# Linear attention plus gated FFN on one core: the V projection becomes a Gram product, gate/up becomes row-tiled, and every engine's order is written by hand

## The chip, the cores and the metric

The kernel runs on one core of one Trainium2 chip. The metric is device time in microseconds (us), the median of the runs of a kernel. Engines are named as the profile names them: PE (TensorE matmul), PEld (TensorE weight load), DVE (VectorE), ACT (ScalarE), POOL (GpSimd), SP (SyncE, which here issues the DMAs; SPq is its queue).

## The reference, cut to what matters

```python
x = A_x                                   # [1, 2048, 576] bf16
xn = layernorm(x)                         # no scale, no shift
q, k, v = heads(xn @ wqkv)                # 32 heads of 18 columns, D = 576
phi = lambda t: where(t > 0, t + 1, exp(t)) + 1e-6
kv  = einsum("bhsd,bhse->bhde", phi(k), v)        # per head 18 x 18
z   = einsum("bhsd->bhd", phi(k))
o   = (phi(q) @ kv) / (phi(q) @ z + 1e-6)
out = x + o @ wo + (gelu(xn @ w_gate) * (xn @ w_up)) @ w_down    # F = 4608
```

The feed-forward part is by far the larger: 576 x 4608 twice and 4608 x 576 once, for 2048 rows.

## The kernel before

The 2048 rows are 16 tiles of 128 (the K/V stage) and 4 chunks of 512 (all else). Each tile is normalised, transposed and projected to K and V; per-head products accumulate in two PSUM banks. Then come Q for all chunks, and for each chunk a gate/up stage and a down stage. A scheduler decides the order in which instructions of different parts stand on each engine, and pools hand out buffers and PSUM banks. In the code, phi of a value t comes in three steps: Relu of -t and Exp on ACT give exp(min(t, 0)), a max on DVE gives max(t, 0) plus the small constant, and an add joins them.

```python
def phi(ps_ap, out_ap, rows, cols, add_eng):
    e = awork.tile(...)
    nc.scalar.activation(out=e, in_=ps_ap, func=ACT.Relu, scale=-1.0)
    nc.scalar.activation(out=e, in_=e, func=ACT.Exp, scale=-1.0)
    a = awork.tile(...)
    nc.vector.tensor_scalar(out=a, in0=ps_ap, scalar1=0.0, scalar2=EPS_ATT, op0=ALU.max, op1=ALU.add)
    add_eng.tensor_tensor(out=out_ap, in0=e, in1=a, op=ALU.add)

def layernorm_transpose(n):
    # 2 bn_stats, bn_aggr on DVE; Ln, Exp on ACT -> rstd            [cut]
    nc.vector.tensor_scalar(out=xn[:, 0:D], in0=xt, scalar1=mv[:, 0:1], scalar2=rstd, subtract, mult)
    nc.vector.tensor_scalar(out=xn[:, D:DX], in0=xt[:, 512:D], ...)  # the tail, once more, 64 columns
    # 5 transposes on PE, one copy to xnT on DVE                     [cut]

def k_project(n):      # per half: 5 matmuls of 288 columns, then phi with the add on POOL
def v_project(n):      # per half: 5 matmuls of 288 columns, then a copy on ACT
def kv_accumulate(n, pk, v):   # 5 matmuls of at most 133 columns into kv_ps0, kv_ps1

for n in range(2, NS):
    if n + 1 < NS:
        layernorm_transpose(n + 1)
    pk = k_project(n)
    pending.append((n, pk, v_project(n)))
    if len(pending) > KV_SKEW:
        kv_accumulate(*pending.pop(0))
# [cut: the rest of kv, Q for 20 units of 5 matmuls of 512 columns]

class _GuBatch:                      # r = 2 blocks f of 128 columns of w_gate and w_up
    def full(self, first):           # rows 0..511 of the contraction, 128 rows each
        for i in range(self.r):
            for (pst, wsb) in ((self.g[i], self.wg), (self.u[i], self.wu)):
                for kt in range(4):
                    nc.tensor.matmul(pst[:], lhsT=wsb[:, kt, fcol], rhs=xnT[:, kt, self.cs], ...)
    def pairs(self, first):          # rows 512..575: g on rows 0..63 and u on rows 64..127 of the array
        for i in range(self.r):
            nc.tensor.matmul(self.g[i][:], lhsT=self.wr[0:64, fcol],   rhs=xnT[0:64, 4, self.cs], ...)
            nc.tensor.matmul(self.u[i][:], lhsT=self.wr[64:128, fcol], rhs=xnT[64:128, 4, self.cs], ...)

def gu_double_batch(sc, f0, r):
    a.full(True); a.pairs(False); a.geglu()      # [cut: allocation]
    b.pairs(True); b.full(False); b.geglu()
```

Of the kernel before, what the change touches and what calls it, by code (L numbers as in the profile page):

```python
# [12 lines left out]
PSUM = bass.MemoryType.PSUM  # L13

P = 128
S = 2048
# [3 lines left out]
DA = DH + 1  # L20
# [7 lines left out]
DX = D + 64  # L28
# [4 lines left out]
CW = 7 * DA  # L33
# [7 lines left out]
KV_SKEW = 2  # L41
# [14 lines left out]
def kernel(  # L56
# [15 lines left out]
    x_flat = A_x.flatten_outer_dims()  # L72
    out_flat = out.flatten_outer_dims()
    x_view = x_flat.rearrange("(n p) d -> p n d", p=P)
    out_view = out_flat.rearrange("(n p) d -> p n d", p=P)
# [4 lines left out]
    dwork = ctx.enter_context(tc.tile_pool(name="dwork", bufs=2))  # L80
    fpool = ctx.enter_context(tc.tile_pool(name="ffn", bufs=1))
    fwork = ctx.enter_context(tc.tile_pool(name="fwork", bufs=3))
    psum = ctx.enter_context(tc.tile_pool(name="psum", bufs=8, space=PSUM))

    def bank(name):
        return psum.tile([P, 512], F32, name=name, tag="ps")

    def bank_bf16(name):
        return psum.tile([P, 8, P], BF16, name=name, tag="ps")
# [3 lines left out]
    if NWARM:  # L93
        warm = bank("warm")
        for _ in range(NWARM):
            nc.tensor.matmul(warm[:, 0:P], lhsT=ident[:], rhs=ident[:], start=True, stop=True)
    eps_ln = const.tile([P, 1], F32, name="eps_ln")
    nc.vector.memset(eps_ln[:], EPS_LN)
    nc.scalar.preload_act_table_set("natural_log_exp_and_others")

# [5 lines left out]
    kv18 = persist.tile([P, NCH, CR], BF16, name="kv18")  # L106
    kvT = persist.tile([P, NCH, CR], BF16, name="kvT")

    hT = fpool.tile([P, NF, SC], BF16, name="hT")
# [4 lines left out]
    def load_gu_block(f0, r):  # L114
        c0, c1 = f0 * P, (f0 + r) * P
        w = r * P
        wg = wg_bufs.next()
        wu = wu_bufs.next()
        wr = wr_bufs.next()
        nc.sync.dma_start(wg[:, :, :w], B_w_gate[0:512, c0:c1].rearrange("(kt p) c -> p kt c", p=P))  # L120
        nc.sync.dma_start(wu[:, :, :w], B_w_up[0:512, c0:c1].rearrange("(kt p) c -> p kt c", p=P))
        nc.sync.dma_start(wr[0:64, :w], B_w_gate[512:576, c0:c1])
        last = nc.sync.dma_start(wr[64:128, :w], B_w_up[512:576, c0:c1])
        return wg, wu, wr, last

    attn_cm = tc.tile_pool(name="attn", bufs=1)
    apool = attn_cm.__enter__()
    awork_cm = tc.tile_pool(name="awork", bufs=3)
    awork = awork_cm.__enter__()
    asmall_cm = tc.tile_pool(name="asmall", bufs=4)  # L130
    asmall = asmall_cm.__enter__()

    x_src = {}

    def load_x(n0, cnt):
        if cnt == 1:
            t = awork.tile([P, D], BF16, name="xs", tag="xs", bufs=2)
            nc.sync.dma_start(t[:], x_view[:, n0, :])
            x_src[n0] = t[:]
        else:  # L140
            t = awork.tile([P, 4, D], BF16, name="xg", tag="xg", bufs=2)
            nc.sync.dma_start(t[:, :cnt, :], x_view[:, n0:n0 + cnt, :])
            for i in range(cnt):
                x_src[n0 + i] = t[:, i, :]

    wqkv_sb = apool.tile([P, KT, 3 * D], BF16, name="wqkv_sb")
    nc.vector.memset(wqkv_sb[64:128, 4, :], 0.0)

    def load_wqkv_main(c0, c1):
        nc.sync.dma_start(wqkv_sb[:, 0:4, c0:c1], A_wqkv[0:512, c0:c1].rearrange("(kt p) c -> p kt c", p=P))  # L150

    load_x(0, 1)
    load_x(1, 1)
    load_wqkv_main(D, D + HALF)
    nc.sync.dma_start(wqkv_sb[0:64, 4, D:3 * D], A_wqkv[512:576, D:3 * D])
    load_wqkv_main(D + HALF, 2 * D)
    load_x(2, 2)
    load_wqkv_main(2 * D, 2 * D + HALF)
    load_wqkv_main(2 * D + HALF, 3 * D)
    load_wqkv_main(0, D)  # L160
    nc.sync.dma_start(wqkv_sb[0:64, 4, 0:D], A_wqkv[512:576, 0:D])
    load_x(4, 4)
    X_LATER = {3: (8, 4), 7: (12, 4)}

    bmask = const.tile([P, 7, DA], F32, name="bmask")

    def build_bmask():
        nc.gpsimd.memset(bmask[:], 1.0)
        nc.gpsimd.affine_select(
            out=bmask[:], in_=bmask[:], compare_op=ALU.is_ge, fill=0.0,  # L170
            base=0, pattern=[[-DH, 7], [0, DA]], channel_multiplier=1,
        )
        nc.gpsimd.affine_select(
            out=bmask[:], in_=bmask[:], compare_op=ALU.is_ge, fill=0.0,
            base=DH - 1, pattern=[[DH, 7], [0, DA]], channel_multiplier=-1,
        )

    NVB = KV_SKEW + 2
    v_bufs = _Ring([apool.tile([P, H, DA], BF16, name=f"v{i}") for i in range(NVB)])
    pk_bufs = _Ring([apool.tile([P, D], BF16, name=f"pk{i}") for i in range(NVB)])  # L180
    for t in v_bufs.tiles:
        nc.gpsimd.memset(t[:, :, DH:DA], 1.0)

    kv_ps = [bank("kv_ps0"), bank("kv_ps1")]

    def kv_accumulate(n, pk, v):
        for c in range(NCH):
            rows = DH * HCH[c]
            q0 = DH * HOFF[c]
            nh = HCH[c]  # L190
            h0 = HOFF[c]
            b = c // 3
            col = (c - 3 * b) * CW
            first_in_bank = (n == 0 and c in (0, 3))
            nc.tensor.matmul(
                kv_ps[b][:rows, col:col + nh * DA], lhsT=pk[:, q0:q0 + rows],
                rhs=v[:, h0:h0 + nh, :].rearrange("p h e -> p (h e)"),
                start=first_in_bank, stop=(n == NS - 1 and c in (2, 4)), skip_group_check=True,
            )

    def phi(ps_ap, out_ap, rows, cols, add_eng):
        e = awork.tile([P, SC], F32, name="phi_e", tag="phi_e")
        nc.scalar.activation(out=e[:rows, :cols], in_=ps_ap, func=ACT.Relu, scale=-1.0)
        nc.scalar.activation(out=e[:rows, :cols], in_=e[:rows, :cols], func=ACT.Exp, scale=-1.0)  # L204
        a = awork.tile([P, SC], F32, name="phi_a", tag="phi_a")
        nc.vector.tensor_scalar(  # L206
            out=a[:rows, :cols], in0=ps_ap, scalar1=0.0, scalar2=EPS_ATT, op0=ALU.max, op1=ALU.add,
        )
        add_eng.tensor_tensor(out=out_ap, in0=e[:rows, :cols], in1=a[:rows, :cols], op=ALU.add)

    def layernorm_transpose(n):
        xt = x_src.pop(n)
        stats = asmall.tile([P, 2, nc.vector.BN_STATS_DIM], F32, name="stats")
        xr = xt.rearrange("p (a b) -> p a b", a=2)
        for a_ in range(2):
            nc.vector.bn_stats(out=stats[:, a_, :], in_=xr[:, a_, :])  # L216
        mv = asmall.tile([P, nc.vector.BN_AGGR_DIM], F32, name="mv")
        nc.vector.bn_aggr(out=mv[:], in_=stats[:])
        rstd = asmall.tile([P, 1], F32, name="rstd")
        nc.scalar.activation(out=rstd[:], in_=mv[:, 1:2], func=ACT.Ln, bias=eps_ln[:], scale=1.0)  # L220
        nc.scalar.activation(out=rstd[:], in_=rstd[:], func=ACT.Exp, scale=-0.5)
        xn = awork.tile([P, DX], BF16, name="xn")
        nc.vector.tensor_scalar(  # L223
            out=xn[:, 0:D], in0=xt, scalar1=mv[:, 0:1], scalar2=rstd[:],
            op0=ALU.subtract, op1=ALU.mult,
        )
        nc.vector.tensor_scalar(
            out=xn[:, D:DX], in0=xt[:, 512:D], scalar1=mv[:, 0:1], scalar2=rstd[:],
            op0=ALU.subtract, op1=ALU.mult,
        )  # L230
        tp = bank_bf16("tp_x")
        for kt in range(KT):
            nc.tensor.transpose(tp[:, kt, :], xn[:, kt * P:(kt + 1) * P], ident[:])  # L233
        nc.vector.tensor_copy(out=xnT[:, :, n * P:(n + 1) * P], in_=tp[:, 0:KT, :])  # L234

    def k_project(n):
        ts_ = slice(n * P, (n + 1) * P)
        pk = pk_bufs.next()
        for hf in range(2):
            ps_k = bank("ps_k")  # L240
            for kt in range(KT):
                nc.tensor.matmul(  # L242
                    ps_k[:, :HALF], lhsT=xnT[:, kt, ts_],
                    rhs=wqkv_sb[:, kt, D + hf * HALF: D + (hf + 1) * HALF],
                    start=(kt == 0), stop=(kt == KT - 1),
                )
            phi(ps_k[:, :HALF], pk[:, hf * HALF:(hf + 1) * HALF], P, HALF, nc.gpsimd)
        return pk

    def v_project(n):  # L250
        ts_ = slice(n * P, (n + 1) * P)
        v = v_bufs.next()
        for hf in range(2):
            ps_v = bank("ps_v")
            for kt in range(KT):
                nc.tensor.matmul(  # L256
# [7 lines left out]
            )  # L264
        return v

    layernorm_transpose(0)
    layernorm_transpose(1)
    pk0 = k_project(0)
    pk1 = k_project(1)  # L270
# [244 lines left out]
```

## Time and profile before

The first three runs gave a median of 545.75 us (544.07 to 546.41).

| stage of the profiled execution | length, us | what fills it |
|---|---|---|
| K/V tiles, until Q starts | 63.22 | from 40 to 60 us PE without a gap, at the end 3.01 a tile |
| Q | 21.58 | 100 matmuls, one every 0.216 |
| gate/up of chunk 0 | 74.76 | |
| gate/up of chunks 1, 2, 3 | 71.75, 71.70, 71.62 | |
| down of chunk 0, of the others | 41.79, 41.40 | |

The page of the kernel before, its parts on busy time (share of the span, number of instructions) and on the chain that ended last (share of the span by engine):

```profile
PE 528.8 (97%) x3371; PEld 311.4 (57%) x3403; DVE 258.0 (48%) x462; ACT 152.0 (28%) x329; POOL 67.8 (12%) x79
...
PE 92%; DMA 2%; DVE 2%; SPq 1%; issue 1%; POOL 0%; ACT 0%; POOLq 0%; ACTq 0%
```

PE is the bound. Only work taken off PE, or a gap between two of its instructions, can move the time.

The same by stage. Each line is a stretch, its length, the busy time of each engine with the number of instructions, the granted clock, the share of the DMA engines and GB/s:

```profile
core 0: us, PE busy (x) PEld busy (x) DVE busy (x) ACT busy (x) POOL busy (x), PEclk, DMA share, GB/s
0.00:63.22 63.22, 55.07 (x517) 45.31 (x517) 44.87 (x130) 41.50 (x129) 27.11 (x45) 0.95 0.47 125
63.22:84.80 21.58, 21.58 (x103) 13.12 (x102) 19.05 (x31) 19.35 (x34) 12.51 (x10) 1.00 0.00 1
84.80:159.56 74.76, 74.12 (x374) 32.43 (x380) 46.95 (x86) 28.92 (x57) 10.80 (x9) 1.00 0.73 207
159.56:201.35 41.79, 41.73 (x337) 32.85 (x337) 24.08 (x34) 0.69 (x2) 5.80 (x5) 1.00 0.13 37
201.35:273.10 71.75, 71.18 (x354) 30.23 (x361) 23.62 (x37) 20.51 (x36) 0.00 (x0) 1.00 0.51 145
```

In the K/V stage DVE (44.87) and ACT (41.50) have less to do than PE (55.07), but not much less.

The K/V stage in the chain of waits of the kernel before (start, length, engine, output, line, count):

```profile
47.86 1.23 PE ps_k L242 x10
49.09 1.23 PE ps_v L256 x10
...
50.87 1.23 PE ps_k L242 x10
52.09 1.23 PE ps_v L256 x10
```

From one K to the next are 3.01 us: K 1.23, V 1.23, and transposes and kv in the rest. The chain stays on PE: the other engines keep up.

Gate/up in the timeline of the kernel before (start, length, engine, line, operation, output<-inputs), where it changes from 64-row to 128-row matmuls:

```profile
212.85 0.38 PE L400 MATMUL g<-xnT,wr_135 64*128 64x512 bf16 x1
212.85 0.38 PE L402 MATMUL u<-xnT,wr_135 64*128 64x512 bf16 x1
213.07 0.38 PE L400 MATMUL g<-xnT,wr_135 64*128 64x512 bf16 x1
213.07 0.38 PE L402 MATMUL u<-xnT,wr_135 64*128 64x512 bf16 x1
213.38 1.04 PE L392 MATMUL g<-xnT,wg_127 128*128 128x512 bf16 x4
```

Two 64-row matmuls on different halves of the array start together, and such pairs follow each other every 0.22 us, as full matmuls do. But from the last pair to the first full matmul are 0.31 us. (The 0.38 us length is that of one matmul in the pipeline; the spacing of the starts is what a slot costs.)

### The profile page before, as it was taken

To read this page: it belongs to the slowest core of one execution; us is meant where nothing else is said; L and a number is where in the kernel's file an instruction comes from. 1 tells how busy PE (TensorE), PEld (TensorE's weight loads), DVE (VectorE), ACT (ScalarE), POOL (GpSimd) and SP (SyncE) were. 2 spreads that over 40 slices of the span, in tenths; PEclk is the share of its full clock that TensorE was granted. 3 is DMA by queue.
4 is the path that set the end of the run, shared out by engine and by line. 5 is a ranking of instruction groups with operands and counts; after the bars stand their busy time and mean duration, and the time that the engine had idled before them with its cause. 6 is when DMAs were issued, how large, how long until landed. Compare 5 with 4: busy or idle time off the path is not lost.

```text
span 542.6 us, 8817 instructions
## 1 busy us (share of the span) xinstructions
PE 528.8 (97%) x3371; PEld 311.4 (57%) x3403; DVE 258.0 (48%) x462; ACT 152.0 (28%) x329; POOL 67.8 (12%) x79
## 2 busy tenths in 40 slices
PE   5999999999999999999999999999999999999997
PEld 4788764444457774444477744444677644445775
DVE  5996598877248613333288123323683123323101
ACT  3677797223330003223200013223100122322000
POOL 1445465101002100000011000000021000000000
PEclk8999999999999999999999999999999999999999
DMA  8920003897840114554511035545301245540000
GB/s 251 251 78 2 1 2 95 254 257 211 227 135 24 29 34 141 155 145 143 163 52 38 28 103 145 161 137 154 110 23 32 74 136 157 148 127 0 23 18 16
DMA packets 104851, 58.08 MB, mean 107 GB/s; under 512 B 5802, under 2 KB 104746, under 8 KB 104810
## 3 DMA queue, kind: packets, MB, share of 16 engines
q1 hardware_dynamic: 104810, 57.53, 37.6%
q8 instruction: 26, 0.43, 0.4%
q14 instruction: 15, 0.12, 0.1%
HBM read 55.15 MB, written 2.36 MB: 106 GB/s over the span
## 4 chain that ended last, share of the span: by engine, by line
PE 92%; DMA 2%; DVE 2%; SPq 1%; issue 1%; POOL 0%; ACT 0%; POOLq 0%; ACTq 0%
PE acc L468 26%; PE g L392 23%; PE u L392 23%; PE g L400 6%; PE ps_q L332 4%; PE acc L475 4%; DMA xg<-in_A_x_dram 2%; PE ps_k L242 2%; PE ps_v L256 2%; PE ps_den L365 1%; DVE stats L216 1%; DVE phi_a L206 1%; SPq L150 0%; PE tp_x L233 0%; DVE xn L223 0%
## 5 line engine op out<-in xcount | busy, mean ns | idle before, releaser
L409 DVE TENSOR_TENSOR hT<-u,gl 128x512 bf16<-128x512 f32 x144 | 95.7, 686 | 171.9 <-PE u L402 104.2
L408 ACT ACTIVATE gl<-g 128x512 f32<-128x512 f32 x144 | 81.9, 596 | 321.3 <-PE u L402 262.2
L468 PE MATMUL acc<-wd_sb,hT 128*128 128x288 bf16 x1152 | 146.4, 286 | 0.0
L468 PEld LDWEIGHTS <-hT 128*128 128x128 bf16 x1152 | 112.6, 98 | 30.0
L370 DVE RECIPROCAL den_sb<-den_sb 126x128 f32<-126x128 f32 (+3 forms) x100 | 68.0, 746 | 0.7
L371 POOL TENSOR_TENSOR pqT<-pqT,den_sb 126x512 bf16<-126x512 bf16 (+1 forms) x20 | 23.2, 1161 | 298.4 <-DVE den_sb L370 298.4
L480 DVE TENSOR_TENSOR res<-acc,xres 128x288 bf16<-128x288 f32 x32 | 14.6, 457 | 88.3 <-PE acc L475 88.3
L392 PE MATMUL u<-xnT,wu_133 128*128 128x512 bf16 x144 | 37.0, 379 | 0.1
L392 PE MATMUL u<-xnT,wu_131 128*128 128x512 bf16 x144 | 37.0, 379 | 0.1
L392 PE MATMUL u<-xnT,wu_130 128*128 128x512 bf16 x140 | 36.6, 379 | 0.3
L392 PE MATMUL g<-xnT,wg_128 128*128 128x512 bf16 x139 | 36.5, 379 | 0.2
L392 PE MATMUL g<-xnT,wg_127 128*128 128x512 bf16 x136 | 36.0, 380 | 0.7 <-issue 0.5
L392 PE MATMUL u<-xnT,wu_132 128*128 128x512 bf16 x140 | 36.4, 379 | 0.2
L392 PE MATMUL g<-xnT,wg_129 128*128 128x512 bf16 x137 | 36.1, 380 | 0.5 <-issue 0.3
L392 PE MATMUL g<-xnT,wg_126 128*128 128x512 bf16 x140 | 36.4, 379 | 0.1
L242 PE MATMUL ps_k<-wqkv_sb,xnT 128*128 128x288 bf16 x160 | 24.4, 304 | 6.0 <-DVE xnT L234 5.7
L204 ACT ACTIVATE phi_e<-phi_e 128x288 f32<-128x288 f32 (+2 forms) x52 | 26.7, 514 | 1.5
L475 PE MATMUL acc<-m_sb,pqT 126*128 126x288 bf16 (+1 forms) x160 | 24.9, 285 | 0.0
L392 PEld LDWEIGHTS <-wg_127 128*128 128x128 bf16 x144 | 12.6, 98 | 20.7 <-issue 7.9
L392 PEld LDWEIGHTS <-wg_129 128*128 128x128 bf16 x144 | 12.6, 98 | 20.4 <-issue 7.6
L392 PEld LDWEIGHTS <-wu_130 128*128 128x128 bf16 x144 | 14.1, 98 | 17.0
L392 PEld LDWEIGHTS <-wu_131 128*128 128x128 bf16 x144 | 14.1, 98 | 17.0
(96 smaller groups left out, 504.6 us busy)
## 6 DMA issues: line engine op xcount, KB each, us to landing
wd_sb<-in_B_w_down_dram SPq DMA_DIRECT2D x12, 432.0 KB, 4.0
wg_126<-in_B_w_gate_dram SPq DMA_DIRECT2D x18, 256.0 KB, 3.0
wu_130<-in_B_w_up_dram SPq DMA_DIRECT2D x18, 256.0 KB, 4.0
wg_127<-in_B_w_gate_dram SPq DMA_DIRECT2D x18, 256.0 KB, 3.0
wu_131<-in_B_w_up_dram SPq DMA_DIRECT2D x18, 256.0 KB, 3.3
wg_128<-in_B_w_gate_dram SPq DMA_DIRECT2D x18, 256.0 KB, 3.0
wu_132<-in_B_w_up_dram SPq DMA_DIRECT2D x18, 256.0 KB, 3.5
wg_129<-in_B_w_gate_dram SPq DMA_DIRECT2D x18, 256.0 KB, 3.1
```

Of the source, the lines that this page charges most:

```text
L204: nc.scalar.activation(out=e[:rows, :cols], in_=e[:rows, :cols], func=ACT.Exp, scale=-1.0)
L242: nc.tensor.matmul(ps_k[:, :HALF], lhsT=xnT[:, kt, ts_], rhs=wqkv_sb[:, kt, D + hf * HALF: D + (hf + 1) * HALF], start=(kt == 0), stop=(kt ...
L332: nc.tensor.matmul(ps[:rows, :], lhsT=wqkv_sb[:, kt, q0:q0 + rows], rhs=xnT[:, kt, sc * SC:(sc + 1) * SC], start=(kt == 0), stop=(kt == KT ...
L370: nc.vector.reciprocal(out=dsb[:rows, q * w:(q + 1) * w], in_=dsb[:rows, q * w:(q + 1) * w])
L371: nc.gpsimd.tensor_tensor(out=pqT[:rows, c, cs], in0=pqT[:rows, c, cs], in1=dsb[:rows, :], op=ALU.mult)
L392: nc.tensor.matmul(pst[:], lhsT=wsb[:, kt, fcol], rhs=xnT[:, kt, self.cs], start=(first and kt == 0), stop=(not first and kt == 3),)
L400: nc.tensor.matmul(self.g[i][:], lhsT=self.wr[0:64, fcol], rhs=xnT[0:64, 4, self.cs], start=first, stop=not first)
L408: nc.scalar.activation(out=gl[:], in_=self.g[i][:], func=ACT.Gelu_apprx_tanh)
L409: nc.vector.tensor_tensor(out=hT[:, self.f0 + i, :], in0=self.u[i][:], in1=gl[:], op=ALU.mult)
L468: nc.tensor.matmul(a_ps[:, :HALF], lhsT=hT[:, f, j * P:(j + 1) * P], rhs=wd_sb[:, f, hf * HALF:(hf + 1) * HALF], start=(f == 0), stop=False,)
L475: nc.tensor.matmul(a_ps[:, :HALF], lhsT=pqT[:rows, c, ts_], rhs=m_sb[:rows, c, hf * HALF:(hf + 1) * HALF], start=False, stop=(c == NCH - 1),)
L480: nc.vector.tensor_tensor(out=res[:, hf * HALF:(hf + 1) * HALF], in0=a_ps[:, :HALF], in1=xres[:, hf * HALF:(hf + 1) * HALF], op=ALU.add,)
```

## The change

There are three parts.

1. **V becomes a Gram product.** phi(K)^T (xn Wv) = (phi(K)^T xn) Wv. So V is no longer projected; G = xn^T phi(K), 576 x 576, accumulates over the tiles, a column of ones gives z, and Wv is applied once. V's 10 matmuls of 288 columns per tile are 2880 columns, and so is the Gram product: 2304 columns in the K loop and 576 (block row 3) among the Q units. What really goes is V's copy on ACT, the kv matmuls (about 0.3 us a tile) and the serial link K, V, kv.
2. **Gate/up in 64-row tiles only.** 576 = 9 x 64. Each block f takes 18 half-height matmuls, two at a time, nine slots, as many slots as before, but the array is never switched to another tiling mode. After five slots (`p1`) the two row tiles swap the banks that they write (`p2`); a no-op on SP passes the turn.
3. **A fixed order and fixed PSUM banks** in place of the scheduler and the pools. Statistics run several tiles ahead, the 64-column tail of xn is copied by POOL, x stays in SBUF for the residual, the denominators (den) of chunk 0 move into the Q stage, and kv times Wo (`m_stage`) moves into the first down stage.

```diff
-    def v_project(n): ...                       # [cut] 10 matmuls, 2 ACT copies
-    def kv_accumulate(n, pk, v): ...            # [cut] 5 matmuls
+    def ln_norm(n):
+        nc.vector.tensor_scalar(out=xn[:, n, 0:D], in0=x_sb[:, n, :], ...)
+        nc.gpsimd.tensor_copy(out=xn[:, n, D:640], in_=xn[:, n, 512:D])
+    def k_read(n, hf):       # per half: Relu on ACT and max on DVE, both from PSUM bank 5 + hf
+    def k_finish(n):         # Exp on ACT (576 columns), add on POOL
+    def g_accumulate(n, pieces):
+        for kt, ps_ in pieces.items():
+            for b, col, d0, w in ps_:
+                nc.tensor.matmul(ps_all[:m, b, col:col + w], lhsT=xn[:, n, j0:j0 + m], rhs=pk[:, n, d0:d0 + w], ...)
+    for n in range(NS):
+        if n > 0:
+            k_half(n, 0); k_half(n, 1)
+        k_read(n, 0)
+        if n == 0: ln_norm(2)
+        k_read(n, 1)
+        if n == 0: ln_stats(3); ln_rstd(3)
+        if n + 2 < NS: transposes(n + 2)
+        k_finish(n)
+        if n + 2 < NS: tp_copy(n + 2, 0, KT, acopy)
+        if n + 3 < NS: ln_norm(n + 3)
+        if n + 4 < NS:
+            ln_stats(n + 4)          # 2 bn_stats, bn_aggr on DVE
+            ln_rstd(n + 4)           # Ln, Exp on ACT
+        if n >= GLAG: g_accumulate(n - GLAG, G_A)        # GLAG = 2
+        # [cut: loads]
+    q_banks = _Ring([5, 6, 7, 2, 3, 4])
+    # [cut: 20 Q units; among them block row 3 of G, z, den of chunk 0, G times Wv]
+    class _Unit:
+        def p1(self):
+            for kt in (4, 0, 1, 2, 3):
+                self.mm(0, LO, kt, kt == 4, False)
+                last = self.mm(1, HI, kt, kt == 4, False)
+            self.turn = nc.sync.nop()            # waits for `last`
+        def p2(self):
+            for kt in range(4):
+                m = self.mm(1, LO, kt, False, kt == 3)   # the first one waits for the turn
+                self.mm(0, HI, kt, False, kt == 3)
+    def gu_pair(sc, k):
+        for i in range(GUB):                     # two blocks f
+            if blk > 0: load_gu(blk + NWBUF - 1, i)      # two DMA issues on SP
+            u.p1()
+        for i, (b, u) in enumerate(units):
+            u.p2()                               # then gelu on ACT, product on DVE
+    hooks = [{0: lambda: m_stage((0, 1, 2)), 16: lambda: m_stage((3, 4))} if sc == 0 else {}]
```

The turn is needed because of what the Trainium skill says in "TensorEngine Tiling (Array Packing)", Gotcha 1: different row tiles cannot access one PSUM bank at the same time, and software must synchronise them.

## The prediction

> **What bounds it now.** The page gives PE 97% busy and the granted clock 0.994; the chain of waits that ended last is 92% PE. In the timeline one 512-column matmul follows another every 0.216 us and 288-column ones every 0.1225 us (36 in 4.41 us). Stages, from chain and timeline: first real matmul 10.9 us; K/V tiles to 63.2, steadily 3.02 us a tile, PE gapless; Q to 84.8 (100 x 0.216); gate/up of chunk 0 74.8; later gate/up 71.8 each; each down stage about 41.4 (8 x 5.03 plus den), the last 40.2; end.
>
> **What the change does to PE.**
> 1. Gate/up. Before, four f-blocks take 7.98 us though 36 slots x 0.216 is 7.77. The rest is the switches to and from 64-row matmuls: starts 0.31 us apart instead of 0.216. The Trainium skill, "TensorEngine Tiling (Array Packing)", Key Properties, says that changing the tiling mode drains the engine; this trace agrees, at about 0.1 us a switch. The 64-row pairs already start together (within 0.01 us) and follow every 0.216 us, weight loads hidden, so 18 half-height matmuls should take nine slots, 1.94 us per f. A stage becomes 69.9 us, saving 1.9 x 4. The turn-taking through SP should hide: two DMA issues (0.54 + 0.6 us) fit before each turn is needed. I allow 0.5 us at stage starts, where SP waits for the last output, and 1 us in chunk 0, where 1.02 MB per 3.88 us is 263 GB/s against the 255 reached at most.
> 2. V (1.23) and kv (0.3) per tile go; Gram product comes (2304 columns, 0.985 us in the loop, 0.245 us in the Q stage), then 30 small matmuls, about 1.7 us. Net on PE only about -3 us. Loop PE work falls from 3.02 to 2.49 us a tile.
> 3. den of chunk 0 (1.1) and Gram pieces move into Q: Q grows from 21.6 to about 30.3, plus about 1.1 us waiting for the evacuations of the Gram banks and 0.6 at the gate/up start. kv_stage3 becomes m_stage in down 0: +1.2, plus about 1 of bank wait.
>
> **What I think binds the K loop.** The order gives a loop through two engines: relu(n) on ACT, then (the DVE max waits for ACT) max, max, normalise, two bn_stats, aggregate on DVE, then Ln, Exp on ACT, then relu(n+1). Timeline intervals: 0.45 + 0.36 + 0.36 + 0.34 + 0.72 + 0.23 + 0.33 + 0.10 = 2.89 us. So PE idles about 0.4 us a tile until the last four; most of the Gram gain is lost. Startup: wK complete about 6.5 us, but tile 2's statistics wait for x (7.9) and the fixed order puts the second tile's relu at about 14.5. Then relu(12) 46.7, Q starts about 55.5 (63.2 before), gate/up about 87.5 (84.8 before).
>
> **Sum.** +2.7 up to gate/up, -3.9 gate/up 0, +1.6 down 0, -4.0 gate/up 1 to 3: about -3.6 us. I lean slightly lower: 541 us, 8 in 10 within 533 to 549. Faster by over 2% 0.20, within 2% 0.72, slower 0.08.
>
> **What would show it.** Pair starts every 0.216 us and 3.88 us per gate/up pair, no 0.31 gaps; PE waits in the K stage released by ACT and DVE tile period about 2.9; PE wait on g_sb copies at the fourth Q unit.
>
> **What would make it wrong.** K tile period near 2.5: about 4 to 5 us faster. DVE slowed by POOL's longer f32 adds: period over 3.1. SP turns late behind DMA issues, or row-tiled weight loads not hidden: each 0.1 us per pair costs 7 us.

## The result, and the profile after

The kernel after takes 544.44 us (543.65 to 545.23, four runs), the kernel before 544.99 (544.07 to 546.41, four runs). The ratio is 0.9996, with an interval of 0.9971 to 1.002: no difference. A ratio here is the mean time of one kernel's fast runs over that of the other's of the same rounds, so not quite the ratio of the medians quoted. The result lies inside the range that was given, but the forecast gain of nearly 0.9% (541.0 against 545.75) did not come.

The page of the kernel after, the same parts, and the chain by line:

```profile
PE 526.9 (97%) x4532; PEld 314.6 (58%) x4532; DVE 247.4 (46%) x408; ACT 154.1 (28%) x297; POOL 70.1 (13%) x84
...
PE 87%; ACT 4%; POOL 3%; SPq 2%; DVE 2%; DMA 1%; issue 1%; ACTq 0%; DVEq 0%
PE ps_all L478 50%; PE ps_all L549 26%; PE ps_all L350 4%; PE ps_all L554 4%; POOL hT L253 3%; ACT phi_e L245 2%; PE ps_all L268 1%; ACT phi_e L252 1%; DMA wqkv_sb<-in_A_wqkv_dram 1%; PE ps_all L410 1%; PE ps_all L226 1%; SPq L158 1%; SPq L160 1%; DVE stats L193 0%; POOL xn L213 0%
```

PE's share of the chain fell from 92% to 87%. ACT, POOL and SPq took it: the chain now leaves PE in the K loop (ACT phi_e, POOL hT) and in gate/up (SPq L158 and L160, weight loads that SP issues).

The stages of the kernel after, columns as before:

```profile
0.00:57.20 57.20, 46.90 (x416) 37.48 (x417) 35.48 (x101) 38.84 (x97) 26.93 (x44) 0.97 0.45 130
57.20:88.80 31.60, 30.59 (x192) 20.02 (x191) 19.83 (x35) 23.35 (x44) 16.59 (x13) 1.00 0.00 1
88.80:160.05 71.25, 70.90 (x649) 33.29 (x649) 41.74 (x58) 23.64 (x39) 9.21 (x12) 1.00 0.75 216
160.05:203.55 43.50, 43.01 (x345) 33.80 (x343) 24.39 (x34) 3.69 (x11) 5.80 (x5) 1.00 0.04 12
203.55:275.15 71.60, 70.97 (x649) 30.91 (x648) 24.09 (x36) 20.91 (x35) 0.00 (x0) 1.00 0.53 151
```

| stage | before | predicted | after | after - before |
|---|---|---|---|---|
| until Q starts | 63.22 | 55.5 | 57.20 | -6.0 |
| Q | 21.58 | 32.0 | 31.60 | +10.0 |
| gate/up 0 | 74.76 | 70.9 | 71.25 | -3.5 |
| down 0 | 41.79 | 43.4 | 43.50 | +1.7 |
| gate/up 1, 2, 3 together | 215.07 | 211.1 | 213.39 | -1.7 |
| other downs, end | | | | +0.3 |

The last column adds up to +0.8, which is the difference of the two profiled spans (543.4 and 542.6); the medians differ by 0.55 the other way, and single executions of either kernel by more than both. ("Predicted" is worked out from the prediction's sum: 63.2 - 7.7, then 87.5 - 55.5, then before - 3.9, + 1.6, - 4.0.) Up to gate/up the change costs 4.0 us where 2.7 were expected, and chunks 1 to 3 gain 1.7 where 4.0 were expected. These two are the miss.

**One tile of the K loop**, timeline of the kernel after, ACT, DVE and POOL; the bracket is the idle time before an instruction and what ended it (the profile calls the buffer of phi(K) hT, whose memory it borrows):

```profile
30.00 0.69 ACT L245 ACTIVATE phi_e<-ps_all 128x288 f32<-128x288 f32 x2
30.50 0.82 DVE L246 TENSOR_SCALAR phi_a<-ps_all 128x288 f32<-128x288 f32 x2 [0.97 <-ACT phi_e L245]
30.73 0.68 ACT L252 ACTIVATE phi_e<-phi_e 128x576 f32<-128x576 f32 x1
31.24 0.42 DVE L209 TENSOR_SCALAR xn<-x_sb,mv,rstd 128x576 bf16<-128x576 bf16 x1
31.32 0.68 ACT L222 COPY xnT<-ps_all 128x640 bf16<-128x640 bf16 x1
31.49 1.43 POOL L253 TENSOR_TENSOR hT<-phi_e,phi_a 128x576 bf16<-128x576 f32 x1 [1.49 <-ACT phi_e L252]
31.57 0.81 DVE L193 BATCH_NORM_STATS2 stats<-x_sb 128x6 f32<-128x288 bf16 x2
32.42 0.21 DVE L196 BATCH_NORM_AGGREGATE mv<-stats 128x2 f32<-128x12 f32 x1
32.66 0.30 ACT L205 ACTIVATE rstd<-mv,eps_ln 128x1 f32<-128x1 f32 x1 [0.67 <-DVE mv L196]
32.86 0.24 POOL L213 COPY xn<-xn 128x64 bf16<-128x64 bf16 x1
32.99 0.20 ACT L206 ACTIVATE rstd<-rstd 128x1 f32<-128x1 f32 x1
33.10 0.69 ACT L245 ACTIVATE phi_e<-ps_all 128x288 f32<-128x288 f32 x2
```

Read it as a ring: relu at 30.00, max at 30.50, normalise 31.24, statistics 31.57, aggregate 32.42, Ln 32.66, Exp 32.99, next relu 33.10. The period is 3.10 us, and the longest waits in it are DVE's for ACT's relu (0.97) and ACT's for DVE's aggregate (0.67). PE has only 2.49 us of work for a tile here by the prediction's count, so taking V and kv away saved nothing per tile: 3.10 against 3.01. That Q still starts 6.0 us earlier comes from the ends of the stage: the relu of the third tile stands at 17.60 us instead of 20.88 (3.3 gained at the start), the relu of the last tile at 55.87 instead of 60.32 (a further 1.2; over the last three tiles, which have no later statistics to wait for, the mean period is about 2.4 us), and from there to Q are 1.3 us instead of 2.9, since the Gram pieces of the last two tiles now run among the Q units.

Why does the max wait for the relu at all, when both only read? They read the same PSUM bank. The Trainium skill, "PSUM — Partial Sum Buffer", in its section on PSUM bank collisions, says that the compiler's back end adds a dependency between two engines on one bank and quadrant, reads against reads included. This trace agrees: DVE's first max starts 0.50 us after ACT's relu does, and the wait is put down to that relu. No run gives the two readers different banks, so that this rule is the reason is inferred.

**One turn in gate/up**, timeline of the kernel after, SP's queue and the instructions that wait for it:

```profile
219.61 0.38 SPq L157 DMA_DIRECT2D wg<-in_B_w_gate_dram  x1
220.03 1.53 SPq L158 DMA_DIRECT2D wr<-in_B_w_gate_dram  x1
221.67 0.09 PEld L478 LDWEIGHTS <-wu 64*128 64x128 bf16 x1 [0.43 <-SPq L487]
...
222.41 0.51 SPq L161 DMA_DIRECT2D wr<-in_B_w_up_dram  x1
223.04 0.39 PE L478 MATMUL ps_all<-xnT,wu 64*128 64x512 bf16 x1 [0.33 <-SPq L487]
```

Issuing one weight load kept SP for 1.53 us; the turn (L487) stands behind it in SP's queue, and PE waited, at this turn and at the next. In undisturbed pairs matmul pairs follow every 0.216 us and a gate/up pair takes 3.88 us, as predicted. But for 0.1 and 0.3 us at the start of chunk 0, where the turn has no part, every gap lies at the first `p2` matmul of a unit. Added up over the four stages, the profiled execution of the kernel after loses about 4 us more than an execution with punctual turns (experiment e3).

**The Q stage** has one wait, as predicted, at its fourth unit (timeline of the kernel after):

```profile
63.63 1.29 PE L350 MATMUL ps_all<-xnT,wqkv_sb 128*126 128x512 bf16 x5 [1.01 <-ACT phi_e L363]
```

That unit's bank held Gram sums, which ACT and DVE were still copying out. (The profile names ACT's Exp L363, but DVE's last copy out of this bank ends at 63.58 us, and e8, which gives the unit another bank, has no such wait.)

### The profile page after: what moved, and what is told of

Its sections match the earlier page's. It is cut to its first block, busy times and chain, and to the rows that moved or that the text cites. A ratio compares the mean times of both kernels' runs of the same rounds, so it can differ in the third digit from the quotient of the medians.

```text
span 543.4 us, 10754 instructions
## 1 busy us (share of the span) xinstructions
PE 526.9 (97%) x4532; PEld 314.6 (58%) x4532; DVE 247.4 (46%) x408; ACT 154.1 (28%) x297; POOL 70.1 (13%) x84
## 4 chain that ended last, share of the span: by engine, by line
PE 87%; ACT 4%; POOL 3%; SPq 2%; DVE 2%; DMA 1%; issue 1%; ACTq 0%; DVEq 0%
PE ps_all L478 50%; PE ps_all L549 26%; PE ps_all L350 4%; PE ps_all L554 4%; POOL hT L253 3%; ACT phi_e L245 2%; PE ps_all L268 1%; ACT phi_e L252 1%; DMA wqkv_sb<-in_A_wqkv_dram 1%; PE ps_all L410 1%; PE ps_all L226 1%; SPq L158 1%; SPq L160 1%; DVE stats L193 0%; POOL xn L213 0%
## 5 line engine op out<-in xcount | busy, mean ns | idle before, releaser
L478 PE MATMUL ps_all<-xnT,wg 64*128 64x512 bf16 x1152 | 274.6, 376 | 0.0
L478 PE MATMUL ps_all<-xnT,wu 64*128 64x512 bf16 x1152 | 272.7, 376 | 1.3 <-SPq L487 0.8
L522 DVE TENSOR_TENSOR hT<-ps_all,gl 128x512 bf16<-128x512 f32 x144 | 99.6, 692 | 170.8 <-ACT gl L521 170.4
L521 ACT ACTIVATE gl<-ps_all 128x512 f32<-128x512 f32 x144 | 86.1, 598 | 318.4 <-PE ps_all L478 299.0
L478 PEld LDWEIGHTS <-wu 64*128 64x128 bf16 x1152 | 106.2, 94 | 73.3 <-SPq L487 11.4
L549 PE MATMUL ps_all<-wd_sb,hT 128*128 128x288 bf16 x1152 | 146.5, 286 | 0.0
L478 PEld LDWEIGHTS <-wg 64*128 64x128 bf16 x1152 | 106.6, 94 | 66.9 <-issue 0.6
L424 DVE RECIPROCAL den_sb<-den_sb 126x128 f32<-126x128 f32 (+1 forms) x80 | 68.3, 911 | 0.5
L478 PE MATMUL ps_all<-xnT,wr 64*128 64x512 bf16 x288 | 57.7, 376 | 0.1
L253 POOL TENSOR_TENSOR hT<-phi_e,phi_a 128x576 bf16<-128x576 f32 x16 | 22.7, 1420 | 22.9 <-ACT phi_e L252 22.9
L554 PE MATMUL ps_all<-m_sb,pqT 126*128 126x288 bf16 (+1 forms) x160 | 24.9, 285 | 0.0
```

The source lines that it names most:

```text
L253: nc.gpsimd.tensor_tensor(out=pk[:, n, :], in0=e[:], in1=a[:], op=ALU.add)
L424: nc.vector.reciprocal(out=d[:, h:h + P], in_=d[:, h:h + P])
L478: return nc.tensor.matmul(self.outs[i], lhsT=self.lhs(i, rows, kt), rhs=self.rhs(i, rows, kt), start=start, stop=stop, skip_group_check=True,)
L521: nc.scalar.activation(out=gl[:], in_=ps_all[:, b[0], :], func=ACT.Gelu_apprx_tanh)
L522: nc.vector.tensor_tensor(out=hT[:, GUB * k + i, :], in0=ps_all[:, b[1], :], in1=gl[:], op=ALU.mult)
L549: nc.tensor.matmul(acc, lhsT=hT[:, f, j * P:(j + 1) * P], rhs=wd_sb[:, f, hs], start=(f == 0), stop=False,)
```

## The experiments

Ten kernels ran, each against runs of the kernel before on the same chip. Each edit is shown against the kernel after. Two theories stood against each other for the K loop. A: the ring through ACT and DVE sets the period, because the statistics of tile n+4 are asked for in the very tile in which Ln and Exp on ACT need them, ahead of the next relu. B: POOL sets it, because the chain of waits runs through POOL's add (L253) and its copy of the tail (L213). For gate/up the theory is that the turn comes late behind SP's DMA issues; the rival is that row-tiled matmuls are themselves no faster.

| run | median, us | ratio to before | interval |
|---|---|---|---|
| the kernel after | 544.44 | 0.9996 | 0.9971 to 1.002 |
| e1: statistics one tile further ahead | 539.51 | 0.9926 | 0.9911 to 0.994 |
| e2: tail on DVE, after the normalise | 559.3 | 1.0283 | 1.0268 to 1.0299 |
| e2b: tail on DVE, before the normalise | 558.76 | one look | |
| e3: turn through ACT | 540.88 | 0.9948 | 0.9933 to 0.9962 |
| e4: gate/up in the old form | 547.63 | 1.0071 | 1.0053 to 1.0088 |
| e5: Gram product of one tile only (wrong result) | 543.5 | one look | |
| e6: e1, e3 and a later `m_stage` | 535.91 | 0.9839 | 0.9821 to 0.9857 |
| e7: other fix of the K loop, rest as e6 | 535.8 | 0.9838 | 0.9821 to 0.9855 |
| e8: e6 with banks in another order | 534.86 | 0.9827 | 0.9799 to 0.9855 |
| e9: loads behind both turns | 541.9 | 0.9958 | 0.9927 to 0.999 |

### e1: take the statistics out of the ring

```diff
+        if n == 0:
+            ln_stats(4)
         if n + 4 < NS:
-            ln_stats(n + 4)
             ln_rstd(n + 4)
+        if n + 5 < NS:
+            ln_stats(n + 5)
```

> The bn_stats and aggregate of a tile are issued one tile earlier on DVE, so the Ln of ACT no longer waits for the same tile's DVE work. Theory A (the loop relu, max, max, normalise, bn_stats, aggregate, Ln, Exp, relu sets the 3.10 us of a K tile): the tile period falls to 2.5 to 2.7 us, Q starts 5 to 6 us earlier than 57.4, the whole kernel takes about 539 us (ratio to before about 0.990). Rival B (the chain printed by the profile is right and POOL's f32 add followed by its tail copy releases the next relu): the period stays 3.10 within 0.05 and the time stays at 544 within 1.

Measured: 539.51 us, ratio 0.9926, and Q starts at 52.27 instead of 57.21. The two Exps of consecutive tiles in the timeline of e1:

```profile
31.25 0.68 ACT L252 ACTIVATE phi_e<-phi_e 128x576 f32<-128x576 f32 x1
...
33.74 0.68 ACT L252 ACTIVATE phi_e<-phi_e 128x576 f32<-128x576 f32 x1
```

They are 2.49 us apart, and the next interval is 2.83; over eight tiles the mean period is 2.66, against 3.10. No work was removed; the Ln merely finds its statistics ready. Theory A is shown to hold for the wait that mattered. POOL's add and its copy are the same as in the kernel after, so B would have left the period alone. With the ring cut, PE is nearly the bound again: it is busy for 20.61 of the 21.29 us of eight tiles (19.62 to 40.91).

### e2 and e2b: take POOL's copy away

```diff
-        nc.gpsimd.tensor_copy(out=xn[:, n, D:640], in_=xn[:, n, 512:D])
+        nc.vector.tensor_scalar(out=xn[:, n, D:640], in0=x_sb[:, n, 512:D], scalar1=mv[:, n, 0:1],
+                                scalar2=rstd[:, n:n + 1], op0=ALU.subtract, op1=ALU.mult)
```

In e2 the new instruction stands after the 576-column normalise, in e2b ahead of it.

> The 64-column tail of xn is written by DVE (a second normalise, as in the kernel before) instead of a copy on POOL behind the f32 add. Theory A: the DVE part of the loop grows by about 0.21 us, so the period of a K tile rises from 3.10 to about 3.3 and the kernel to about 546.5 us. Rival B (POOL add and tail copy release the relu): the tail copy leaves the chain, the period falls by 0.2 or more to 2.9 or less, the kernel gets about 2 us faster.

Measured for e2: 559.3 us, ratio 1.0283, period 4.39 us. B had forecast a shorter loop, and with POOL's copy gone it did not get shorter; but as the edit also put a long hold on DVE, e2 alone does not refute B. That e1 does. The size is a miss. In the kernel before, the same 64-column instruction takes 0.29 us in 14 of 16 tiles; here, in the timeline of e2:

```profile
30.42 1.43 POOL L256 TENSOR_TENSOR hT<-phi_e,phi_a 128x576 bf16<-128x576 f32 x1 [2.96 <-ACT phi_e L255]
30.51 1.38 DVE L213 TENSOR_SCALAR xn<-x_sb,mv,rstd 128x64 bf16<-128x64 bf16 x1
...
34.81 1.43 POOL L256 TENSOR_TENSOR hT<-phi_e,phi_a 128x576 bf16<-128x576 f32 x1 [2.96 <-ACT phi_e L255]
```

The tail starts 0.09 us after POOL's add and ends with it, 0.04 us later. It was held, not slow. The ring grew by 1.29 us (4.39 - 3.10), nearly the whole of the tail's 1.38, as A has it for time added to DVE's part. Over eleven tiles that makes 14.2 us, about what e2 lost against the kernel after (14.9 by the medians).

> As e2, with the two DVE instructions swapped: the 64-column tail first, then the 576-column normalise, so that both can start before POOL's f32 add. In e2 the tail started 0.09 us after the add and took 1.38 us, ending with it; the same instruction takes 0.29 in the kernel before. If DVE was locked out by the add (and not slow for another reason), both now run at full speed: tile period about 3.3 (3.10 plus 0.2), kernel about 546.5 us. If the tail is slow in itself, the period stays near 4.4 and the time near 559.

Measured for e2b: 558.76 us (one look), period 4.50. The numbers are those foreseen for a tail that is slow in itself, yet the timeline of e2b shows that it is not:

```profile
32.83 0.29 DVE L209 TENSOR_SCALAR xn<-x_sb,mv,rstd 128x64 bf16<-128x64 bf16 x1
33.03 1.61 DVE L213 TENSOR_SCALAR xn<-x_sb,mv,rstd 128x576 bf16<-128x576 bf16 x1
33.08 1.40 POOL L256 TENSOR_TENSOR hT<-phi_e,phi_a 128x576 bf16<-128x576 f32 x1 [3.10 <-ACT phi_e L255]
```

Now the tail takes its 0.29 us, and it is the normalise that takes 1.61 us instead of 0.42; it ends at 34.64, POOL's add at 34.48. In e2 it was the instruction that starts 0.09 us after POOL's add, in e2b the one recorded 0.05 us before it; each is held until that add ends. This is what the Trainium skill says in "SBUF — State Buffer", "Who interferes with whom": DVE and GpSimd share a port pair under an exclusive lock, `tensor_scalar` can enter a mode that takes it, and the second to issue blocks fully. In the kernel after the normalise starts 0.25 us ahead of the add and is done in 0.42; and bn_stats, which runs beside the add, takes 0.81 for two, 0.44 each, as it does with no POOL instruction beside it (0.44 in both kernels). The hold could have been seen before the change: in the kernel before, two of the 16 tails take 0.78 us and two of the 16 normalises 0.78 and 0.82, and each of these four starts 0.06 to 0.18 us after an add of POOL and ends within 0.2 us after it. So the kernel after owes some of its speed to where one 0.42 us instruction happens to stand.

### e3: pass the turn through ACT

```diff
-            self.turn = nc.sync.nop()
+            self.turn = nc.scalar.nop()
```

> The turn between the row tiles is passed through ACT's queue instead of SP's, where it stands behind two weight DMA issues. Theory: nearly all gaps of the gate/up stages at slots 18 and 27 (3.9 us summed over the four stages in the trace) are the turn arriving late; they go, the later gate/up stages fall from 71.6, 70.7 and 71.0 to about 70.0, the kernel takes about 540.5 us (ratio about 0.993). Rival (the weights themselves come late, or DMA bandwidth): the gaps stay, and the time stays at 544 within 1.

Measured: 540.88 us, ratio 0.9948. Two gate/up stages of e3, chunks 1 and 2:

```profile
202.42:272.40 69.98, 69.98 (x649) 31.45 (x648) 24.04 (x36) 20.91 (x35) 0.00 (x0) 1.00 0.54 155
313.88:383.90 70.02, 70.02 (x649) 31.45 (x648) 24.08 (x36) 20.91 (x35) 0.00 (x0) 1.00 0.55 155
```

Compare 71.60 in the kernel after and 71.75 before. PE is busy for the whole of these stages, and no gap is left at any turn; 0.3 us remain in chunk 0, where the second unit waits for a bank. The prediction's 69.9 us for a stage is what row tiling gives when the turn is punctual. The gain is 2.6 us by the ratios and 3.6 by the medians; in the profiled executions the four stages lose about 4. The size of the loss differs between executions: the runs of the kernel after spread over 1.58 us, those of e3 over 0.29.

### e4: gate/up in the old form, all else as after

```diff
-            u.p1()                         # and p2(), and the turn
+        for step in (("full", "pair") if k % 2 == 0 else ("pair", "full")):
+            for b, u in units:             # full: 128-row matmuls kt 0..3 for g and u
+                ...                        # pair: kt 4, g on rows 0..63, u on rows 64..127   [cut]
```

> All of the change but the gate/up form: full-height matmuls with the 64-row pairs together, two mode switches per four f-blocks, no turns. If the drains at mode switches are what row tiling saves, each gate/up stage returns to about 71.8 us as before, where the changed kernel has 70.7 to 71.6 because of late turns: the kernel takes 546 to 547.5 us, 2 to 3 more than the changed one. If row tiling saves nothing, the time stays at 544 within 0.5; if it costs, the time falls.

Measured: 547.63 us, ratio 1.0071. A gate/up stage takes 71.98 us again. So, on the rest of the new kernel, row tiling is worth 1.0071 - 0.9996 = 0.75% (4 us) with the turn on SP and 1.0071 - 0.9948 = 1.23% (6.7 us) with a punctual turn. It also shows what the other parts of the change are worth together: they lose 0.7%.

### e5: take the Gram work out of the K loop

```diff
-        if n >= GLAG:
+        if n == GLAG:
```

The result is wrong (relative error 0.028): all but one tile's Gram sums are left out of the loop.

> Wrong result on purpose: the Gram matmuls of tiles 1 to 13 are left out, so PE has about 1.5 us of work per K tile instead of 2.49. Theory A (the ACT and DVE loop sets the pace): the period stays 3.10 within 0.03 and the kernel takes 543 to 545 us, at most 1.5 less than the changed kernel (from the last four tiles). Rival (PE's own work or its weight loads set the pace): the period falls by up to 1 us a tile, the time by 8 us or more.

Measured: 543.5 us (one look). The relus of two consecutive tiles in the timeline of e5:

```profile
29.81 0.69 ACT L245 ACTIVATE phi_e<-ps_all 128x288 f32<-128x288 f32 x2
...
32.91 0.69 ACT L245 ACTIVATE phi_e<-ps_all 128x288 f32<-128x288 f32 x2
```

PE has about 1.0 us less to do per tile, and the period stays 3.10 us to the last digit. PE does not set it. Only the last tiles and those after the loop gain: Q starts at 55.43.

### e9: leave the turn on SP, but put the loads behind it

```diff
         for i in range(GUB):
-            if blk > 0:
-                load_gu(blk + NWBUF - 1, i)
             u.p1()
+        if blk > 0:
+            load_gu(blk + NWBUF - 1, 0)
+            load_gu(blk + NWBUF - 1, 1)
```

> The changed kernel with the turn left in SP's queue, but the four weight DMA issues moved behind the two turns of a pair. If the turn is late only because it stands behind DMA issues in SP's order, the gaps at slots 18 and 27 go as in e3: about 541 us, ratio 0.994 to 0.995, later gate/up stages 70.0. If a turn through SP is slow in itself, the gaps stay and the time is 544.

Measured: 541.9 us, ratio 0.9958. In chunks 1 to 3 every gap is gone, pair after pair at 3.88 us; in chunk 0, where the slices of w_down are issued from SP too, two late turns remain (pairs of 4.56 and 3.95 us). So the fault is not SP as such but what stands in SP's queue ahead of the turn.

Why an issue at times takes 1.5 us instead of about 0.5 is open. There is a correlation: in the kernel after, from gate/up on, all 13 issues longer than 0.9 us overlap in time with a packet of the instruction queue q8, which moves 16 KB at a time, and only 17 of the 288 others do; in e3 it is 10 of 10 and 20 of 291, in the kernel before 4 of 4 and 21 of 325. The instruction queue, in the page's list of DMA queues of the kernel before (packets, MB, share), and then of the kernel after:

```profile
q8 instruction: 26, 0.43, 0.4%
```

```profile
q8 instruction: 35, 0.57, 0.5%
```

Row tiling has more instructions (4532 matmuls against 3371), so more of these packets. No run changed the packets alone, so this stays a correlation.

### e6 and e7: both repairs together

e6 is e1, e3 and

```diff
-        hooks = [{0: lambda: m_stage((0, 1, 2)), 16: lambda: m_stage((3, 4))} if sc == 0 else {}]
+        hooks = [{16: lambda: m_stage((0, 1, 2)), 24: lambda: m_stage((3, 4))} if sc == 0 else {}]
```

> e1 (statistics one tile ahead), e3 (turn through ACT), and the m_stage hooks of the first down stage moved from f 0 and 16 to f 16 and 24, so that they do not wait for the last gate/up banks (0.44 us wait on hT plus issue gaps in the trace). If the gains add: 544.4 - 4.9 - 3.6 - 1.4 (late turns that e1 had more of) - 0.7 = about 534 us, ratio to before 0.981 to 0.984. If late turns and the K loop shared the same slack, 537 or more.

Measured: 535.91 us, ratio 0.9839. By the medians e1 gained 4.9 us and e3 3.6; the down stage of chunk 0 went from 43.50 to 42.69 us in the profile, as `m_stage` no longer waits for its turn at the start of the stage. Together that makes 9.3, and 8.5 were measured; by the ratios it is 3.8, 2.6 and 0.8, together 7.2, against 8.6. So within the noise the gains add, as gains in different stages should. The forecast of about 534 was 2 us too low.

e7 leaves the statistics where they are and moves Ln and Exp instead, behind the relus of the next tile:

```diff
         if n == 0:
             ln_stats(3)
-            ln_rstd(3)
+        elif n + 3 < NS:
+            ln_rstd(n + 3)
         ...
+        if n == 0:
+            ln_rstd(3)                # after tp_copy
         if n + 4 < NS:
             ln_stats(n + 4)
-            ln_rstd(n + 4)
```

> e6 with another way to cut the loop: instead of the statistics one tile ahead, the Ln and Exp of a tile wait on ACT until after the next tile's two relus. The loop through aggregate and Ln no longer holds the relu: period 2.5 to 2.7 as in e1; and in the first tiles the relu of tile 1 comes at about 13 us instead of 14.6. So about 1 us faster than e6: 533. If the startup is held by something else (PE at half clock, POOL), it equals e6 within 0.5 us.

Measured: 535.8 us, ratio 0.9838, the same as e6. The extra gain hoped for did not come: the relu of the second tile did stand 1.0 us earlier (13.39 against 14.41 us), but Q started no earlier in the profiled run (53.65 against 52.12). The period was not the 2.5 to 2.7 expected but 2.80 over eight tiles, against 2.66 in e6, and over the loop that takes back the head start. That the ring can be cut at either of two places with the same time for the kernel supports A.

### e8: another order of banks

```diff
-    q_banks = _Ring([5, 6, 7, 2, 3, 4])
+    q_banks = _Ring([5, 6, 7, 4, 3, 2])
-    banks = _Ring(list(range(8)))
+    banks = _Ring([0, 1, 2, 5, 6, 7, 4, 3])
```

The rest is e6. The bank whose Gram sums are copied out first is now used first.

> e6 with another order of PSUM banks: the fourth Q unit takes the bank whose Gram piece is evacuated first, and the first gate/up units take banks that the last Q units do not use. In the trace of e6 the wait at the first gate/up pair is 0.8 us; in that of the changed kernel the wait of the fourth Q unit is 1.0. If both are only bank waits, 1.8 us go: about 534 us, ratio to before near 0.981. If the PE merely waits later for the same ACT and DVE work, it stays within 0.5 us of e6 (535.9).

Measured: 534.86 us, ratio 0.9827. The Q stage of e6, and then that of e8:

```profile
52.12:83.69 31.57, 30.56 (x190) 19.98 (x188) 19.80 (x35) 23.32 (x44) 16.57 (x13) 1.00 0.00 1
```

```profile
54.17:84.51 30.34, 30.34 (x190) 20.05 (x188) 19.70 (x35) 23.31 (x44) 16.55 (x13) 1.00 0.00 1
```

PE is now busy for the whole of the stage: the waits of Q, 1.2 us, were waits for banks. Gate/up of chunk 0 fell too, from 70.51 to 70.04. The timed difference is nearer 1 us. In the profile e8's K stage ended 2.05 us later than e6's, although its code is the same; its first K matmul, which waited for the weights, started at 7.00 us instead of 6.52, and PE ran at half the clock from 17.3 to 20.7 us, inside the K loop, where e6 had such a stretch from 10.5 to 13.9, among the first tiles. Half-clock stretches of that sort are what the Trainium skill describes in "TensorE: Matmul & The Clock Gate", Part 1, with a window that does not start with the kernel; the traces agree, with 3.41 us in each of the two. The start of the kernel thus varies between executions by more than this edit is worth. e8 is the fastest version seen, 1.7% below both kernels; whether it beats e6 is not settled, since the intervals overlap.

## Why the prediction was wrong, and where it was right

**Right: what binds.** The ring through ACT and DVE was named, link by link, from the instruction order alone, as was the start (second relu at about 14.5 us; measured 14.57), the mode switch (a stage of 69.9 us; 69.98 in e3), the down stage of chunk 0 (43.4; 43.50), the wait at the fourth Q unit (1.1; 1.01) and the length of the Q stage (32.0; 31.6). It also saw that V's replacement by a Gram product saves PE little.

**Wrong: two terms of the sum.** Both mechanisms had been named; the first was mis-sized, and the second is an overlap that was counted on and did not hold.

1. The step "0.45 + 0.36 + 0.36 + 0.34 + 0.72 + 0.23 + 0.33 + 0.10 = 2.89". The ring took 3.10. From relu to max were 0.50 us, not 0.45; the two bn_stats took 0.85 from start to start of the next step, not 0.72; the other links together the rest. The 0.85 are 0.37 and 0.48, the latter to the aggregate that needs the result of the bn_stats just before it; in the kernel before, 0.36 (half of 0.72) is the step from a bn_stats to an instruction that does not need it. It is not DVE slowed by POOL's add, which the prediction listed: in e2 no add runs beside this step, and it takes 0.47. Over eleven tiles 0.21 us a tile make about 2.3 us; the relu of tile 12 came 1.9 later than predicted (48.59 against 46.7) and Q 1.7. e5 shows that it was not PE, e1 and e7 that it was the ring, and e1 that it was not POOL's copy.
2. The step "The turn-taking through SP should hide: two DMA issues (0.54 + 0.6 us) fit before each turn is needed. I allow 0.5 us at stage starts ... and 1 us in chunk 0". The typical issue does fit; the rare one does not. An issue of up to 1.65 us makes a turn late, in the middle of a stage, in every chunk. Chunks 1 to 3 together took 213.4 us where 211.1 had been allowed. The loss was listed under "what would make it wrong" (SP turns late behind DMA issues), but with no size in the sum. e3 and e9 show the cause from two sides.

The two make about 4 us together, against a forecast of -3.6 from the sum. A third, smaller fault: having a sum of -3.6, the prediction leaned about 1.2 us further down to 541.0, with nothing measured for it; and the median of the kernel before itself came down by 0.8 with one more run.

**Where the expected gain went.** Of the gain in gate/up (7.6 us as an estimate from 1.9 a stage; 6.7 between e4 and e3) the late turns took back 2.6 to 4. What remained was spent in front: Q's start came 6.0 us earlier, but the Q stage grew by 10.0 because it took over den and Gram work, and down 0 by 1.7. The K loop gave nothing per tile, as its period went from PE's 3.01 to the ring's 3.10.

**A trap in the profile.** The chain of waits of the kernel after names POOL's add and copy on the way round the K loop. Both were only the last to report: POOL's copy ended at about the moment at which ACT's Exp of rstd ended (33.10 and 33.19 in the timeline above). e1 shortened the loop without touching POOL; e2 took the copy from POOL, and the loop got longer.

## What to carry to other kernels

When work is taken from the engine that binds, work out the ring that remains: follow the fixed order from an instruction of tile n through every engine to the same instruction of tile n+1, with durations and the gaps between them; the step that is asked for at the last moment, here the statistics, goes one tile further ahead and costs nothing. A signal that another engine needs on time must not stand in a queue behind work with a long tail, even when the median fits; look at the longest issue, not the typical one. And before moving an instruction to another engine, look at what it will run beside: 0.29 us became 1.38.

## What the Trainium skill lacked or had wrong

- No page that I found, "DMA: Bandwidth & Descriptors" among them, gives a figure for how long one issue occupies SP: about 0.5 us in the median here, and up to 1.65. "Runtime: NRT & Kernel Launch", in its section on instruction fetch, calls the cost of crossing a 16 KiB block mostly hidden; here all 13 long issues after the start of gate/up overlap with a 16 KB packet of the instruction queue, against 17 of 288 others. What ties them is open, so this does not show the page to be wrong.
- "TensorEngine Tiling (Array Packing)" says that a mode switch drains the engine, but gives no cost: it is about 0.1 us here (0.31 us from start to start instead of 0.216). Nor does it say what the synchronisation of row tiles can cost: 2.6 to 4 us of 544 when the turn goes through SP's queue, about nothing through ACT's.
- "SBUF — State Buffer" says that whichever of DVE and GpSimd issues first takes the shared ports. The recorded starts do not tell which that was: in e2b the normalise is recorded 0.05 us ahead of POOL's add and was the one held (1.61 us instead of 0.42), while 0.25 us ahead, in the kernel after, it was not.
